# K and V of two chunks side by side in the array, a reordered prologue, and a tail that streams FFN products before out_proj

## The chip, the cores and the metric

The kernel runs on one core of one Trainium2 chip. Its time is the device time of that core in microseconds, as the median of a few runs; one further execution was recorded by the hardware profiler. Engines are PE (TensorE, matmuls), PEld (its weight loads), DVE (VectorE), ACT (ScalarE), POOL (GpSimd) and SP (SyncE, which issues most DMAs). Each engine takes its instructions strictly in the order written.

## What is computed

```python
x = A_x                                            # 1 x 2048 x 512
g = _sigmoid((x * gate_w).sum(-1, keepdims=True))
q = (x @ wq).reshape(B, S, 32, 16)                 # 32 heads of 16
k = x @ wk ; v = x @ wv                            # one K and V for all heads
p = _softmax(einsum("bhqd,bkd->bhqk", q, k) * 16 ** -0.5)
a = einsum("bhqk,bkd->bhqd", p, v).reshape(B, S, 512) @ wo
b = _silu(x @ w1) @ w2                             # w1: 512 x 1792
return g * a + (1 - g) * b
```

## The kernel before

Everything is float32 outside; inside, an operand is split into an upper and a lower float16 half (`split`: ACT makes the upper, DVE the lower), and a product is three matmuls (`product3`: upper x upper, upper x lower, lower x upper).

**Prologue** (`first_pass`). x comes in 4 chunks of 512 rows (`xn`). `T(c, t)` transposes 128 rows on PE and splits them into `xs`. `K(c)` multiplies a chunk by K's, V's and the gate's weights together (`wkvs`, 64 columns) into bank "pk", 12 matmuls 64 columns wide. `parts`/`place` split K and spread it over the partitions into `KT`; `v_rows`/`V` transpose V into `VF`. `W` splits the first half of wq, `Q(n)` makes one block of 128 columns of q for a chunk, writes it to memory (`qd`), and `load_q` reads it back rearranged into `qb`, by six DMAs plus two with the shift rows. `shift` makes a bound per head and query (`kab` times |q|) that stands in for the row maximum. `pieces_.step()` splits one piece of w1, w2, wq or wo, 128 x 512, that a DMA put into one of two buffers `raw`; a step asks for the load of a later piece into the buffer that it has emptied.

**Stream** (`attention`). 32 rounds (4 chunks, 4 blocks of 128 columns of q, 2 halves) of 16 steps, 512 steps; a step has two "scores" of 8 matmuls (`S<-qb,KT`, 32 columns each, eight tiles of the array at once). So there are 1024 scores, each followed by one exponential of 128 x 1024 on ACT (`P<-S`, L1180), in two pairs of PSUM banks: score n needs exponential n-2 done. The sums P x V are taken in one of two ways: native float32 (`pv<-P,VF`), or as two cheap products (`P,VP` and `L,VP`) for which DVE first makes `L` (L1199, 128 x 2048). Between scores a planner (`serve`, `put`, `f_slot`, with costs such as `SLOT` for a group of 8 matmuls) lays the FFN's and the output projection's products into banks "pm", of which there are two, and DVE's work by due times; the order is fixed when the program is built. `need(w, g)` puts all missing steps of a weight group on DVE at once.

The first scores are placed by hand, letter by letter, from `FIRST`: S is a score, E one matmul of an "early" Q block (blocks 4 and 5, 12 matmuls of 128 x 512 each, evicted by DVE at L929/L930), B is `bound` for block 1, which fetches the next FFN block and its "pm" bank first.

**Tail**. After the last score come the last sums, the last paired FFN products (48 matmuls at L835), the normalisation of the last round on DVE (`norm_a`, ending in `O`), then 72 full-height matmuls (L839): 12 of out_proj and 60 of the FFN, each block in a "pm" bank and evicted by DVE into `acc` (L809), which SP stores.

Of the kernel before, what the change touches and what calls it, by code (L numbers as in the profile page):

```python
# [31 lines left out]
FIRST = "EEEEEEEEEESEESEEEESEEEESBEEEE"  # L32
# [15 lines left out]
def kernel(  # L48
# [21 lines left out]
    nc = tc.nc  # L70
# [145 lines left out]
    def masks(cst):  # L216
# [6 lines left out]
        mj = cst.tile([16, 8, 16], F32)  # L223
        nc.gpsimd.iota(mj, pattern=[[0, 8], [1, 16]], base=0, channel_multiplier=-1, allow_small_or_imprecise_dtypes=True)
        sel_k = cst.tile([16, 8, 16], F32)
        nc.vector.tensor_scalar(flat(sel_k), flat(mj), 0.0, None, op0=OP.is_equal)
        selA = cst.tile([16, 8, 16], F16)
        selB = cst.tile([16, 8, 16], F16)
        nc.vector.memset(selA, 0.0)
        nc.vector.memset(selB, 0.0)  # L230
        for b in (0, 2, 4, 6):
            nc.vector.tensor_copy(selA[:, b], sel_k[:, b])
        for b in (1, 5):
            nc.vector.tensor_copy(selB[:, b], sel_k[:, b])
        part = cst.tile([128, 1], F32)
        nc.gpsimd.iota(part, pattern=[[0, 1]], base=0, channel_multiplier=1, allow_small_or_imprecise_dtypes=True)
        pm = cst.tile([128, 1], F32)
        nc.vector.tensor_scalar(pm, part, 64.0, -64.0, op0=OP.is_ge, op1=OP.mult)
        nc.vector.tensor_tensor(pm, pm, part, op=OP.add)
        rm = cst.tile([128, 2], F32)  # L240
# [15 lines left out]
    def load_q(q, c, o, rb, shifts):  # L256
# [3 lines left out]
        for f in range(2):  # L260
            b = 64 * f
            nc.sync.dma_start(q[b:b + 16], v[f, rb][:, :, 0])
            nc.sync.dma_start(q[b + 16:b + 32], v[f, rb][:, :, 0])
            nc.sync.dma_start(q[b + 32:b + 48], v[f, rb][:, :, 1])
            if shifts:
                nc.sync.dma_start(q[b + 48:b + 48 + shifts], u[f, rb][0:shifts])
        return q
# [22 lines left out]
    def loads(sb, q_cols):  # L290
# [7 lines left out]
        xn = []  # L298
        for c in range(NCH):
# [24 lines left out]
    def k_places(pk, k1, k2, selA, selB):  # L324

        nc.tensor.matmul(pk, flat(selA), k1, start=True, stop=False)
        nc.tensor.matmul(pk, flat(selB), k2, start=False, stop=True)
# [59 lines left out]
    def first_pass():  # L387
        with ExitStack() as pro:
# [8 lines left out]
            vr = sb.tile([64, S], F32)  # L397
            mx = sb.tile([16, NCH], F32)
            mxa = sb.tile([16, 1], F32)
            k_to = KS / (SX * SKV)  # L400
            ks = {}

# [4 lines left out]
            def K(c):  # L407
                ks[c] = bank("pk", 2)
                kv_product(ks[c], wkvs, c)

            def parts(c):
                pk = ks[c]
                k1, k2 = ks[c, "k"] = [wk_.tile([16, 512], F16, name=n) for n in ("k1", "k2")]
                nc.scalar.activation(k1, pk[0:16], AF.Copy, scale=k_to)
                absmax(mx[:, c:c + 1], k1)
                if c == NCH - 1:
                    nc.vector.tensor_reduce(mxa, mx, axis=AX.X, op=OP.max)
                nc.vector.scalar_tensor_tensor(k2, pk[0:16], k_to, k1, op0=OP.mult, op1=OP.subtract)

            def v_rows(c):  # L420
                nc.scalar.activation(vr[32:64, c * 512:c * 512 + 512], ks[c][32:64], AF.Copy)

            def place(c):
                pk = ps.tile([128, 512], F32, name="pt", bufs=4)
                k_places(pk, *ks[c, "k"], selA, selB)
                nc.scalar.activation(KT[:, c * 512:c * 512 + 512], pk, AF.Identity, bias=m_one)
# [24 lines left out]
            def shift(n, pu):  # L451
# [4 lines left out]
                if n == 0:  # L456

                    for p in range(2):
                        nc.sync.dma_start(qb_[0][48:113:64, p], s1[32 * p:32 * p + 3:2])
                return q_shift(o, c, s1)  # L460

            split(wkvs[:, 0], wkvs[:, 1], wkv, SKV)
            for m, a, n in (M_K, 0, 16), (M_V, 32, 16), (M_G, 48, 1):
                absmax(mxs[:, m:m + 1], wkvs[:, 0, :, a:a + n], AX.XY)
            T(0, 0, 1, 2, 3)
# [3 lines left out]
            T(1, 0, 1)  # L469
            K(0)  # L470
            T(1, 2, 3)
            T(2, 0)
            parts(0)
            T(2, 1)
            v_rows(0)
            K(1)
            place(0)
            T(2, 2, 3)
            T(3, 0)
            V(0)  # L480
            parts(1)
            T(3, 1)
            v_rows(1)
            W(0)
            W(1)
            K(2)
            pieces_.step(by_scalar=True)
            pieces_.step(by_scalar=True)
            place(1)
            T(3, 2, 3)  # L490
            V(1)
            parts(2)
            for _ in Q(0, pq):
                pass
            load_q(qb_[0], 0, 0, 0, 0)
            v_rows(2)
            pieces_.step(by_scalar=True)
            K(3)
            parts(3)
            place(2)  # L500
            q1 = Q(1, bank("pq", 1))
            next(q1)
            next(q1)
            prep = bank("pk", 2)
            nc.tensor.matmul(prep[:, 0:1], flat(sel_k), mxa, start=True, stop=True)
            kv_ = sb.tile([128, 1], F32)
            nc.vector.tensor_copy(kv_, prep[:, 0:1])
            nc.vector.tensor_scalar(kab, hmask, kv_, 2.0 ** -10 * (1 + 2.0 ** -9), op0=OP.mult, op1=OP.mult)
            v_rows(3)
            place(3)  # L510
            note = shift(0, bank("pk", 2))
            pieces_.step()

            lo = sb.tile([16, 2], F32)
            nc.vector.tensor_scalar(lo[:, 0:1], mxa, 0.5, None, op0=OP.is_lt)
            nc.vector.tensor_scalar(lo[:, 1:2], mxa, 6e4, None, op0=OP.is_gt)
            nc.vector.tensor_tensor(mxs[0:16, M_KK:M_KK + 1], lo[:, 0:1], lo[:, 1:2], op=OP.max)
            V(2)
            V(3)
            nc.vector.tensor_copy(VF[:, :, 0:16], pv_[:, :, 0:16])  # L520
            note()
            for _ in q1:
                pass
            sigmoid(pv_, -1.0 / (SX * SKV))
# [11 lines left out]
    def second_pass():  # L536
        with ExitStack() as pro:
# [61 lines left out]
            nc.tensor.matmul(prep[:, 0:1], flat(sel_k), km[0:16], start=True, stop=True)  # L599
# [137 lines left out]
    def attention(ctx, scale_of, t_scale, shifts, split_pieces, chores, q_todo, bounds, early, gates_, later):  # L737
# [356 lines left out]
        def norm_a(i, pv, rb, key):  # L1094
# [13 lines left out]
            def joined():  # L1108
# [10 lines left out]
                end = dve[0] + 1.9 if late else on_pool(4.0, dve[0]) + 2  # L1119
                put(0.84, end, end + 4, quotient)  # L1120

            def quotient():
# [5 lines left out]
                if rb:  # L1128
                    put(0.7, dve[0], dve[0] + 4, turned)
# [256 lines left out]
        while T_.cur or T_.going:  # L1386
            serve(pe[0])
            if not T_.going:
                nc.tensor.drain()
                for t in list(tasks):  # L1390
                    if t is T_.evicted:
                        do(t)
# [44 lines left out]
```

## Time and profile before

| what | us |
|---|---|
| median of 3 runs (lowest, highest) | 1075.2 (1071.62, 1076.59) |
| profiled execution, device time | 1073.23 |
| its span, first to last instruction | 1071.4 |
| first score on PE | 38.80 |
| last exponential ends | 1038.82 |
| last matmul ends | 1064.68 |
| last eviction by DVE ends | 1065.47 |

All times in the text count from the span's start. A row of a timeline is start, length, engine, line, operation, output<-inputs and count; the bracket at its end is the idle time of the engine before it and what ended it. A row of stretches has the stretch, its length, the busy time of each engine, the granted PE clock as a share of full speed, the DMA engines' share and GB/s.

### The profile page before, as it was taken

How to read it: one execution, taken by the hardware profiler on the slowest of the kernel's cores; microseconds unless marked ns; L12 is line 12 of the kernel's file. 1: busy time of each engine (PE TensorE's matmuls, PEld its weight loads, DVE VectorE, ACT ScalarE, POOL GpSimd, SP SyncE). 2: the span in 40 equal slices, each digit the busy share in tenths (PEclk: the TensorE clock that was granted, in tenths of full speed). 3: DMA queues.
4: the chain of work that ended last, by engine and by line, in shares of the span. 5: the costliest groups of instructions: out<-in, count | busy, mean ns of one | idle time of the engine just before them, and what ended most of it. 6: DMA issues, size and time to landing. Idle time of an engine off the chain costs nothing.

```text
span 1071.4 us, 65086 instructions
## 1 busy us (share of the span) xinstructions
PE 1023.1 (95%) x30610; PEld 564.2 (53%) x30610; DVE 916.6 (86%) x838; ACT 999.7 (93%) x1121; POOL 471.2 (44%) x388
## 2 busy tenths in 40 slices
PE   8999999999999999999999999999999999999996
PEld 5465454455555545455555555555555555555452
DVE  6799989999999998788797878888889898889784
ACT  5799999999999999999999999999999999999980
POOL 1034345324352373634744335465475267374620
PEclk9999999999999999999999999999999999999998
DMA  5421211100000100000000010000000010000001
GB/s 199 135 61 49 70 41 54 51 12 22 8 18 31 31 22 11 12 19 16 12 22 11 12 60 12 19 7 22 12 11 11 12 47 8 12 11 12 4 5 42
DMA packets 23079, 32.90 MB, mean 31 GB/s; under 512 B 5137, under 2 KB 13074, under 8 KB 22802
## 3 DMA queue, kind: packets, MB, share of 16 engines
q1 hardware_dynamic: 22050, 27.54, 8.4%
q8 instruction: 241, 3.95, 1.6%
q0 software_dynamic: 320, 1.05, 0.3%
q14 instruction: 36, 0.29, 0.1%
q10 hardware_dynamic: 432, 0.07, 0.0%
HBM read 20.12 MB, written 8.52 MB: 27 GB/s over the span
## 4 chain that ended last, share of the span: by engine, by line
PE 38%; ACT 35%; DVE 13%; issue 8%; POOL 4%; DMA 1%; ACTq 0%; SPq 0%; DVEq 0%; POOLq 0%
ACT P L1180 33%; PE pm L835 13%; PE pv L1278 12%; PE S L1174 9%; DVE L L1199 7%; PE pm L839 2%; ACT e L849 2%; POOL T L1109 1%; POOL U L1111 1%; DVE e L854 1%; PE pt L316 1%; DVE acc L809 1%; POOL T L1112 1%; POOL H L856 0%; POOL U L1116 0%
## 5 line engine op out<-in xcount | busy, mean ns | idle before, releaser
L1180 ACT ACTIVATE P<-S 128x1024 f32<-128x1024 f32 x1024 | 959.6, 1079 | 24.4 <-PE S L1174 22.7
L1199 DVE TENSOR_TENSOR L<-P 128x2048 f16<-128x2048 f32 x245 | 606.8, 2491 | 35.8 <-ACT P L1180 35.2
L1174 PE MATMUL S<-qb,KT 50*32 50x512 f16 x8192 | 435.0, 380 | 13.5 <-ACT P L1180 11.0
L1174 PEld LDWEIGHTS <-KT 50*32 50x32 f16 x8192 | 191.6, 89 | 244.5 <-issue 161.1
L1278 PE MATMUL pv<-P,VF 64*32 64x512 f32 (+1 forms) x5360 | 298.2, 503 | 0.0
L835 PE MATMUL pm<-xs,w1s 64*32 64x512 f16 x5376 | 263.7, 375 | 2.3 <-DVE e L854 1.1
L835 PE MATMUL pm<-w2s,H 64*32 64x512 f16 x4896 | 249.2, 375 | 4.9 <-DVE acc L807 2.0
L1109 POOL TENSOR_TENSOR T<-T,U 128x512 f32<-128x512 f32 x31 | 83.8, 2704 | 275.4 <-DVE U L1104 275.4
L856 POOL CAST H<-e 128x512 f16<-128x512 f32 x56 | 57.7, 1030 | 205.9 <-DVE e L854 204.3
L835 PEld LDWEIGHTS <-w1s 64*32 64x32 f16 x5376 | 116.1, 92 | 53.3 <-issue 14.9
L835 PEld LDWEIGHTS <-H 64*32 64x32 f16 x4896 | 106.2, 92 | 46.5 <-issue 6.3
L1278 PEld LDWEIGHTS pv<-P,VF 64*32 64x32 f32 x5360 | 104.7, 106 | 37.4 <-issue 6.6
L857 POOL TENSOR_TENSOR H<-e,H 128x512 f16<-128x512 f32 x56 | 108.8, 1943 | 4.5
L1278 PE MATMUL pv<-P,VP 64*32 64x512 bf16 x1952 | 108.1, 388 | 1.2 <-DVE U L1104 0.6
L1278 PE MATMUL pv<-L,VP 64*32 64x512 f16 x1952 | 103.3, 375 | 3.1 <-DVE L L1199 2.8
L1278 PEld LDWEIGHTS <-VP 64*32 64x32 f16 x3904 | 67.8, 93 | 45.1 <-issue 20.9
L835 PE MATMUL pm<-xs,wqs 64*32 64x512 f16 x1152 | 83.9, 375 | 1.1 <-DVE e L854 1.0
L854 DVE SCALAR_TENSOR_TENSOR e<-e,pm 128x512 f32<-128x512 f32 x56 | 38.3, 683 | 43.2 <-ACT e L849 42.9
L835 PE MATMUL pm<-wo_s,O 64*32 64x512 f16 x1440 | 68.3, 382 | 3.2 <-DVE acc L809 1.8
L1116 POOL TENSOR_TENSOR U<-U 128x48 f32<-128x48 f32 (+1 forms) x62 | 57.4, 925 | 2.4
L809 DVE SCALAR_TENSOR_TENSOR acc<-pm,g,acc 128x512 f32<-128x512 f32 x48 | 35.7, 744 | 14.6 <-PE pm L839 8.0
L1111 POOL TENSOR_TENSOR U<-T,mu 128x96 f32<-128x96 f32 x31 | 45.5, 1468 | 2.4
(175 smaller groups left out, 623.6 us busy)
## 6 DMA issues: line engine op xcount, KB each, us to landing
qb<-qd SPq DMA_DIRECT2D x192, 32.0 KB
raw<-in_B_w_dram SPq DMA_DIRECT2D x22, 256.0 KB
xn<-in_A_x_dram SPq DMA_DIRECT2D x8, 512.0 KB
out_dram<-acc SPq DMA_DIRECT2D x16, 256.0 KB
qd<-qx SPq DMA_DIRECT2D x12, 256.0 KB
raw<-in_B_w_dram POOLq DMA_DIRECT2D x4, 256.0 KB, 3.1
raw<-in_A_wo_dram SPq DMA_DIRECT2D x4, 256.0 KB
qb<-sh SPq DMA_DIRECT2D x62, 2.0 KB
```

Of the source, the lines that this page charges most:

```text
L809: nc.vector.scalar_tensor_tensor(a, po, gate[:, n:n + 1], a, op0=OP.mult, op1=OP.add)
L835: nc.tensor.matmul(self.bank[32 * m:32 * m + 32], l(i, rows, 32 * m), r(j, rows), start=first, stop=last)
L854: nc.vector.scalar_tensor_tensor(e, e, 1.0, ph, op0=OP.add, op1=OP.mult)
L856: nc.gpsimd.tensor_copy(H[:, 0], e)
L857: nc.gpsimd.tensor_tensor(H[:, 1], e, H[:, 0], op=OP.subtract)
L1109: eng.tensor_tensor(T, T, U, op=OP.add)
L1111: eng.tensor_tensor(z[:, :, 1:1 + DIGITS], T3[:, :, 17:17 + DIGITS], mu[:, :, 1:].to_broadcast([128, 16, DIGITS]), op=OP.mult)
L1116: eng.tensor_tensor(first, first, second, op=OP.add)
L1174: nc.tensor.matmul(sc[32 * m:32 * m + 32, f], KT[b:b + 50, k0:k0 + 32], qtile[i][b:b + 50, j], start=True, stop=True)
L1180: nc.scalar.activation(P[:, 2 * j:2 * j + 2], sc, AF.Exp, scale=scale_of(c, o))
L1199: nc.vector.tensor_tensor(L[s], P, upper(P), op=OP.subtract)
L1278: nc.tensor.matmul(pvs[i][h][32 * j:32 * j + 32, cols], a[r], b[r, j, cols], start=start, stop=rest == n)
```

## The change

1. **K and V.** `K(a)` takes chunks 2a and 2a+1: chunk 2a into columns 0 to 63 of the array (rows 0 to 63 of the bank), chunk 2a+1 into columns 64 to 127, alternating matmul by matmul. There are 48 matmuls as before, in 24 pairs. Splitting K, the absolute maximum and V's rows are done once for a pair, and V is turned by 8 plain matmuls instead of 16 transposes. The masks `sel_k`, `selA`, `selB` cover 128 partitions, and POOL makes selA and selB.
2. **The prologue's order.** wq is loaded between chunks 1 and 2 of x. Ten transposes come before the first K pair. Half of the six loads of `qb` for round 0 are issued by POOL, one of the two shift rows by ACT. Two of the four places of K are evicted by DVE. Two steps of w1 are made instead of four, both with ACT.
3. **The first scores.** `FIRST` begins with a score, and B stands after eleven early products instead of twenty.
4. **The tail.** Products are taken in the stream's order, in a ring of four halves of the scores' banks and two "pm" banks; out_proj comes when `O` is due by the plan.

```diff
-FIRST = "EEEEEEEEEESEESEEEESEEEESBEEEE"
+FIRST = "SEESEEESEEESEEESBEEESEEESEEESEEEE"
...
+            if c == 1:
+                nc.sync.dma_start(wqr, by_row(wq)[:, :, :q_cols])
             xn.append(t_)
-        wqr = sb.tile([128, KD, q_cols], F32)
-        nc.sync.dma_start(wqr, by_row(wq)[:, :, :q_cols])
...
-            def K(c):
-                ks[c] = bank("pk", 2)
-                kv_product(ks[c], wkvs, c)
...
+            def K(a):
+                pk = ks[a] = bank("pk", 2)
+                for kt in range(KD):
+                    for n, (i, j) in enumerate(((0, 0), (0, 1), (1, 0))):
+                        for h in range(2):
+                            c = 2 * a + h
+                            nc.tensor.matmul(pk[64 * h:64 * h + 64], wkvs[:, i, kt], xs[:, j, kt, c * 512:c * 512 + 512],
+                                             start=kt == n == 0, stop=kt == KD - 1 and n == 2)
...
-            def V(c):
-                for t in range(4 * c, 4 * c + 4):
-                    nc.tensor.transpose(pv_[:, t], vr[32:64, t * 128:t * 128 + 128], ident_[0][32:64, 32:64])
+            def V(a):
+                at = ident_[0].rearrange("p (h q n) -> p h q n", h=2, q=2)[:, :, 1]
+                for t in range(4):
+                    nc.tensor.matmul(pv_[:, 8 * a + t:8 * a + t + 5:4], vr[:, a, t * 128:t * 128 + 128], at, start=True, stop=True)
...
+            T(0, 0, 1)
             split(wkvs[:, 0], wkvs[:, 1], wkv, SKV)
+            T(0, 2, 3)
+            T(1, 0, 1, 2, 3)
...
+            T(2, 0, 1)
+            W(0)
+            W(1)
+            K(0)
+            T(2, 2, 3)
+            T(3, 0, 1, 2)
+            upper_k(0)
+            T(3, 3)
+            q0 = Q(0, pq)
...
+            load_q(qb_[0], 0, 0, 0, 0, nc.gpsimd)
+            K(1)
+            upper_k(1)
...
-        while True:
-            while tasks:
-                do(min(tasks, key=lambda t: t[0]))
-            o = ahead.pop() if ahead else fetch()
-            if o is None:
-                break
-            for n in range(o.n):
-                o.whole(n, n == 0, n == o.n - 1)
-            force(o.evict(o.bank))
+        def spaces():
+            while True:
+                for _ in range(2):
+                    sc = pS.tile([128, 2, 512], F32, name="S")
+                    yield sc[:, 0]
+                    yield sc[:, 1]
+                yield pM.tile([128, 512], F32, name="pm")
+                yield pM.tile([128, 512], F32, name="pm")
+
+        space = spaces()
+        while not ended[0] or tasks:
+            serve(pe[0])
+            o = ahead.pop() if ahead else next(seq, 0)
+            if o == 0:
+                ended[0] = True
+                while tasks:
+                    do(min(tasks, key=lambda t: t[0]))
+            elif o is None:
+                pe[0] += 0.05
+            else:
+                if not hasattr(o, "bank"):
+                    o.bank = next(space)
+                for n in range(o.n):
+                    o.whole(n, n == 0, n == o.n - 1)
+                    pe[0] += SLOT
+                o.evict(o.bank)
```

**What moves on DVE at the first early block.** `qs` is Q1's lower half, `raw_79` and `raw_80` are the two buffers of w1's pieces (L197 makes an upper half, L198 a lower), and `O<-pm` is the eviction of the first early block. Before:

```order
L197 TENSOR_SCALAR w1s<-raw_80 128x512
L198 SCALAR_TENSOR_TENSOR w1s<-raw_79,w1s 128x512
L198 SCALAR_TENSOR_TENSOR w1s<-raw_80,w1s 128x512
L515 TENSOR_SCALAR lo<-mxa 16x1
L516 TENSOR_SCALAR lo<-mxa 16x1
L517 TENSOR_TENSOR mxs<-lo 16x1
L520 COPY VF<-pv 128x16x16
L385 TENSOR_REDUCE um<-s_477 64x1
L119 SCALAR_TENSOR_TENSOR qs__508<-pq,qs__508 128x512
L929 TENSOR_SCALAR O<-pm 128x512
L930 SCALAR_TENSOR_TENSOR O<-pm,O 128x512
```

In the changed kernel, where the eviction's lines are L938 and L939:

```order
L198 SCALAR_TENSOR_TENSOR w1s<-raw_79,w1s 128x512
L119 SCALAR_TENSOR_TENSOR qs__477<-pq,qs__477 128x512
L137 TENSOR_REDUCE mxs<-wkvs 128x1 x3
L197 TENSOR_SCALAR w1s<-raw_79 128x512
L198 SCALAR_TENSOR_TENSOR w1s<-raw_80,w1s 128x512
L198 SCALAR_TENSOR_TENSOR w1s<-raw_79,w1s 128x512
L197 TENSOR_SCALAR w1s<-raw_80 128x512
L198 SCALAR_TENSOR_TENSOR w1s<-raw_80,w1s 128x512
L938 TENSOR_SCALAR O<-pm 128x512
L939 SCALAR_TENSOR_TENSOR O<-pm,O 128x512
```

Five steps of w1 now stand between Q1's half and the eviction; the first of them (L197 on raw_79) needs a third piece loaded by POOL, the fourth (L197 on raw_80) a fourth piece loaded by SP. The "pm" banks are handed out in turn: the first early block, then the FFN block that B fetches, then the second early block, whose first matmul (the thirteenth E) therefore waits for L939.

**What moves on SP at the same place.** `qd_0_91` is Q1's block on its way to memory, `qb_82` the queries of round 1. Before:

```order
L445 DMA qd_0_91<-qs__508 128x1024
L262 DMA qb_82<-qd_0_83 16x2x512
L263 DMA qb_82<-qd_0_83 16x2x512
L264 DMA qb_82<-qd_0_83 16x2x512
L266 DMA qb_82<-sh_0_84 1x2x512
...
L931 DMA qd_1_85<-O 128x1024
L180 DMA raw_79<-in_B_w_dram 128x512
```

Now:

```order
L458 DMA qd_0_91<-qs__477 128x1024
L262 DMA qb_82<-qd_0_83 16x2x512
L263 DMA qb_82<-qd_0_83 16x2x512
L264 DMA qb_82<-qd_0_83 16x2x512
L266 DMA qb_82<-sh_0_84 1x2x512
...
L180 DMA raw_80<-in_B_w_dram 128x512
L180 DMA raw_79<-in_B_w_dram 128x512
```

At the dots stand the other four loads of `qb_82`. The load of w1's fourth piece (raw_80) stands behind them; before, that piece had come by POOL ahead of them.

**What moves on DVE in the tail.** The last rows of O's chain and the evictions into `acc`; `gg` marks an out_proj block, `g_65` an FFN block. Before:

```order
L809 SCALAR_TENSOR_TENSOR acc<-pm,g_65,acc 128x512
L1124 RECIPROCAL rr<-T 128x16
L1127 TENSOR_TENSOR C<-T,rr 128x16x16
L1133 STREAM_TRANSPOSE T<-C 128x512
L1135 CAST O<-T 128x512
L1136 TENSOR_TENSOR O<-T,O 128x512
L809 SCALAR_TENSOR_TENSOR acc<-pm,gg,acc 128x512 x4
L809 SCALAR_TENSOR_TENSOR acc<-pm,g_65,acc 128x512 x7
```

Now:

```order
L1146 CAST O<-T 128x512
L1147 TENSOR_TENSOR O<-T,O 128x512
L818 SCALAR_TENSOR_TENSOR acc<-S,g_65,acc 128x512
L818 SCALAR_TENSOR_TENSOR acc<-S,gg,acc 128x512
L818 SCALAR_TENSOR_TENSOR acc<-S,g_65,acc 128x512
L818 SCALAR_TENSOR_TENSOR acc<-S,gg,acc 128x512
L818 SCALAR_TENSOR_TENSOR acc<-pm,gg,acc 128x512 x2
L818 SCALAR_TENSOR_TENSOR acc<-S,g_65,acc 128x512 x4
L818 SCALAR_TENSOR_TENSOR acc<-pm,g_65,acc 128x512
```

Two FFN blocks (24 matmuls on PE) now stand ahead of the four out_proj blocks (12), and five behind (36); the matmuls are the same 72.

In the stream the planner, fed with the new start, also lays the sums differently: 239 of 512 steps by the two cheap products and 273 native, before 244 and 268. From the thirteenth early product to score 12 (counted from 0) PE's order holds 12 early products, 8 scores and 4 whole native sums, and the first FFN product comes behind score 12; before, FFN products began after score 8, and by score 12 there were 12 groups of four FFN matmuls and three whole native sums.

More of the change, by code (lines that the diff above doesn't have):

```diff
@@ new lines, in first_pass @@
+            q1 = Q(1, bank("pq", 1))
+            place(0)
+            V(0)
+            next(q1)
+            prep = bank("pk", 2)
+            nc.tensor.matmul(prep[:, 0:2], flat(sel_k)[both], mxa[both], start=True, stop=True)
+            kv_ = sb.tile([128, 1], F32)
+            nc.vector.tensor_reduce(kv_, prep[:, 0:2], axis=AX.X, op=OP.max)
+            nc.vector.tensor_scalar(kab, hmask, kv_, 2.0 ** -10 * (1 + 2.0 ** -9), op0=OP.mult, op1=OP.mult)
+            lower_k(1)
+            place(1)
@@ L472, in first_pass @@
[L472 to L508, printed above, removed]
@@ L1118, in joined @@
                         eng.tensor_tensor(first, first, z[:, :, 3:4], op=OP.add)
-                end = dve[0] + 1.9 if late else on_pool(4.0, dve[0]) + 2
-                put(0.84, end, end + 4, quotient)
+                if late:
+                    dve[0] += 2.1
+                end = dve[0] if late else on_pool(4.0, dve[0]) + 2
+                put(0.7 if late else 0.84, end, end + 4 * (not late), quotient)
             def quotient():
@@ L1128, in quotient @@
                 if rb:
-                    put(0.7, dve[0], dve[0] + 4, turned)
+                    put(0.7, dve[0], dve[0] + 4 * (not late), turned)
             def turned():
```

144 lines of the change are left out of this document (79 added, 65 removed).

## The prediction

> **What bounds the kernel now.** I read the page's busy shares first, then the busy time by stretch, then the waits inside the long middle stretch.
>
> ```profile
> PE 1023.1 (95%) x30610; PEld 564.2 (53%) x30610; DVE 916.6 (86%) x838; ACT 999.7 (93%) x1121; POOL 471.2 (44%) x388
> ```
> ```profile
> 4.67:38.80 34.13, 33.53 (x174) 19.80 (x174) 24.43 (x60) 21.43 (x40) 2.75 (x6) 1.00 0.50 172
> ...
> 38.80:1038.82 1000.02, 967.60 (x30289) 535.19 (x30292) 874.94 (x747) 976.37 (x1079) 462.61 (x357) 1.00 0.09 25
> ...
> 1043.30:1051.60 8.30, 4.54 (x13) 1.53 (x14) 6.30 (x15) 0.00 (x0) 0.00 (x0) 0.79 0.00 1
> 1051.60:1064.70 13.10, 13.08 (x60) 5.75 (x59) 5.16 (x7) 0.00 (x0) 0.00 (x0) 1.00 0.11 41
> ```
>
> After each stretch come its length and the busy time of PE, PEld, DVE, ACT and POOL, then the granted clock. There are three regimes. Until the first scores at 38.80 PE works 33.5 of 34.1 us, so the prologue is PE's. In the stream PE (967.6 of 1000.0) and ACT (976.4) are both nearly full. In the tail PE works only 4.54 of the 8.30 us before 1051.60. Who is late in the stream, the waits tell (total, times, longest):
>
> ```profile
> ACT P L1180 <- PE S L1174: 22.7, 42, 1.4
> ...
> PE S L1174 <- ACT P L1180: 11.0, 30, 1.0
> ```
>
> ACT waits for scores 22.7 us and PE for exponentials 11.0 us: where one limits the other, it is PE two times in three (22.7 of 33.7).
>
> **Term 1, the prologue up to the end of Q1's product.** Scores and exponentials are numbered from 0. The timeline (start, length, engine, line, count):
>
> ```profile
> 11.50 0.38 PE L127 MATMUL pk<-xs,wkvs 128*64 128x512 f16 x1
> 11.71 0.38 PE L128 MATMUL pk<-xs,wkvs 128*64 128x512 f16 x1
> ...
> 36.34 0.38 PE L129 MATMUL pq<-xs,wqs 128*128 128x512 f16 x1
> ...
> 1019.52 0.41 PE L835 MATMUL pm<-wo_s,O 64*32 64x512 f16 x8
> ```
>
> and the chain of waits over the first 60 us:
>
> ```profile
> 13.67 0.61 ACT xs L118
> ...
> 14.30 1.30 DVE xs L119 x2
> 15.60 0.04 issue
> ```
>
> The K/V matmuls start 0.215 us apart, 48 of them 10.3 us. The last row is eight matmuls in eight tiles of the array in 0.41 us, as long as one (0.38). So I take the pairs to run side by side: 24 x 0.215 = 5.2 us, a saving of 5.2 (none, if they don't). V becomes 8 matmuls for 16; I give it nothing. Between 13.67 and 15.64 PE waits 2.0 us for ACT's and DVE's halves of the split; the new order puts ten transposes ahead of the first pair, but then DVE starves while that pair runs, so this is worth 2.0 at best and -1.0 at worst; I take 1. Q1's last matmul ends at 36.34 + 0.38 = 36.72 now, and would end at 30.5 (29.5 to 32.5, or 35.7 with pairs in turn). POOL's sel casts and the second DMA queues lie beside that.
>
> **Term 2, from Q1 to a steady stream.** Here the new order makes a wait. The first scores no longer stand behind ten early products. But the new FIRST puts its B behind eleven early products. B fetches an FFN block, which takes the second "pm" bank and calls `need`, so DVE gets five steps of w1 ahead of the eviction of the first early block. The 13th early product needs that bank, and it stands ahead of score 5. The fourth piece of w1 is loaded through SP, behind Q1's write and eight loads of qb. The price of this chain, from rows of before:
>
> ```profile
> 37.38 0.69 DVE L119 SCALAR_TENSOR_TENSOR qs__508<-pq,qs__508 128x512 f16<-128x512 f32 x1
> 39.79 0.69 DVE L929 TENSOR_SCALAR O<-pm 128x512 f16<-128x512 f32 x1 [1.71 <-PE pm L839]
> 40.52 0.69 DVE L930 SCALAR_TENSOR_TENSOR O<-pm,O 128x512 f16<-128x512 f32 x1
> ...
> 49.28 0.43 DVE L197 TENSOR_SCALAR w1s<-raw 128x512 f16<-128x512 f32 x1 [1.02 <-DMA raw<-in_B_w_dram]
> 49.74 0.69 DVE L198 SCALAR_TENSOR_TENSOR w1s<-raw,w1s 128x512 f16<-128x512 f32 x1
> ...
> 38.10 0.34 SPq L445 DMA_DIRECT2D qd<-qs__508  x1
> ...
> 42.74 0.35 SPq L931 DMA_DIRECT2D qd<-O  x1
> ...
> 46.43 0.33 SPq L180 DMA_DIRECT2D raw<-in_B_w_dram  x1
> ...
> 37.92 0.17 ACT L331 ACTIVATE gg<-pv 128x16 f32<-128x16 f32 x1
> 39.29 1.94 ACT L1180 ACTIVATE P<-S 128x1024 f32<-128x1024 f32 x2 [1.20 <-PE S L1174]
> ...
> 45.17 15.77 ACT L1180 ACTIVATE P<-S 128x1024 f32<-128x1024 f32 x17 [1.36 <-PE S L1174]
> ```
>
> From Q1's last matmul to the end of DVE's half of its split 1.35 (36.72 to 38.07); SP's write and eight loads 4.64 (38.10 to 42.74); the load of a piece 2.85 (46.43 to 49.28); its two DVE steps 1.15 (49.28 to 50.43); the eviction 1.42 (39.79 to 41.21). Sum 11.4, and some 0.4 more because ACT's two w1 halves now stand ahead of Q1's: 11.8. So the 13th early product starts at 30.5 + 11.8 = 42.3. ACT is free for exponentials 1.4 us after Q1 (36.72 to 38.09), with the 0.4 at 32.3, so the first comes 7 us sooner than now (39.29). They run 15.77 / 17 = 0.93 us apart; score 4 needs exponential 2 done, 32.3 + 3 x 0.93 = 35.1, and the 12th early product follows at about 35.5. From there PE stands still for about 7 us, and ACT runs dry behind it.
>
> What a stop does to PE's clock the tail of before shows, in the timeline and in stretches of half a us (clock third from the end):
>
> ```profile
> 1040.52 2.77 PE L835 MATMUL pm<-w2s,H 64*32 64x512 f16 x48
> 1046.83 4.63 PE L839 MATMUL pm<-wo_s,O 128*128 128x512 f16 x12 [3.54 <-DVE O L1135]
> 1051.57 13.11 PE L839 MATMUL pm<-w2s,H 128*128 128x512 f16 x60
> ```
> ```profile
> 1047.50:1048.00 0.50, 0.44 (x2) 0.17 (x3) 0.00 (x0) 0.00 (x0) 0.00 (x0) 0.50 0.00 0
> ...
> 1050.50:1051.00 0.50, 0.50 (x3) 0.25 (x2) 0.24 (x1) 0.00 (x0) 0.00 (x0) 0.72 0.00 0
> 1051.00:1051.50 0.50, 0.46 (x3) 0.10 (x1) 0.50 (x1) 0.00 (x0) 0.00 (x0) 1.00 0.00 0
> ```
>
> After 3.54 us of idling the granted clock stands at 0.50 from 1047.4 to 1050.8, 3.4 us, which loses 1.7 us of work. I charge the stop of 7 us the same 1.7. [...]
>
> From the 13th product to score 12 the new order holds 12 early products, 8 scores and 4 whole native sums. A native sum costs 0.86 us:
>
> ```profile
> 1017.13 1.04 PE L1278 MATMUL pv<-P,VF 64*32 64x512 f32 x16
> 1017.99 0.40 PE L1174 MATMUL S<-qb,KT 50*32 50x512 f16 x8
> ...
> 1038.12 0.42 PE L1278 MATMUL pv<-P,VP 64*32 64x512 bf16 x8
> 1038.34 0.41 PE L1278 MATMUL pv<-L,VP 64*32 64x512 f16 x8
> 1038.56 0.38 PE L835 MATMUL pm<-w2s,H 64*32 64x512 f16 x1
> ```
>
> 20 x 0.215 + 4 x 0.86 = 7.7, with the clock 9.4: exponential 12 starts at about 42.3 + 9.4 + 0.4 = 52.1. Now exponential 4 starts at 45.17, so 12 starts at 45.17 + 8 x 0.93 = 52.6. Of 7 us at score 0, 0.5 us are left at score 12. Bounds: 2.5 us lost to 2.5 us gained, by Q1's end and the clock.
>
> **Term 3, the rest of the stream.** The new order takes 239 steps by the two cheap products and 273 native, for 244 and 268. Each native step costs 0.86 for 0.44 (1038.12 to 1038.56): 5 x 0.42 = 2.1 us of PE. By score 12 the old order has issued 12 groups of FFN matmuls (2.6 us) and three native sums, the new one none and four: 1.7 us more to come. That is 3.8 us more PE work behind the same exponentials. PE is late two times in three: 2.5 us lost. Bounds: nothing, if all of it falls into PE's own waits, to 3.8.
>
> **Term 4, the tail.** PE now ends its paired products at 1040.52 + 2.77 = 1043.3, waits for O, takes 12 + 60 matmuls, and ends at 1051.57 + 13.11 = 1064.7. The new order puts two FFN blocks (24 matmuls, 5.2 us) where the wait was; O is ready 1046.83 - 1043.3 = 3.5 us in, so it hides. The 72 then run without a stop at full clock in 6 half-tiles and banks: 72 x 0.2155 = 15.5 for 21.4 us. Saving 5.9; I take 5.8. DVE's evictions (every 1.3 us at the end as now) stay behind PE. If one bank is late by one eviction, 4.5. What follows PE's end (last eviction, last store) stays.
>
> **Sum.** The profiled execution took 1073.23. It loses 0.5 (term 2 with 1), gains 2.5 (term 3), loses 5.8 (term 4): 1069.4. It lies 2.0 under the median of the three runs, 1075.2, whose range is 1071.6 to 1076.6; from the median the same sum gives 1071.4. I name 1070.4.
>
> **Rivals.**
> A: the stop at the 13th early product is short or absent, since a load lands sooner than 2.85 us after issue or SP is not behind. For: the 2.85 may hold some wait of DVE's. Then exponential 12 comes at 32.3 + 12 x 0.93 = 43.5 at best instead of 52.1; of these 8.6 us I count 7.4, since PE's backlog in term 3 grows with them: 1063. Chance 0.14.
> B: the pairs don't run side by side. Nothing in the trace shows two 64-column tiles at once. All of term 2 shifts by 5.2: 1075.6, no change. Chance 0.07.
> C, the slower side: after the stop PE stays at half clock. One score and three early products then cost 1.72 us for an exponential's 0.93. Each us at half clock loses 0.5. Slower by 0.5% is above 1080.6, 10.2 us over my sum, which holds 1.7 already: it decides from 24 us at half. At 28 us the time is 1070.4 + 14.0 - 1.7 = 1082.7. Against: 1051.00 is back at 1.00 after 3.4 us with PE less dense. Chance 0.07. [...]
>
> **Chances.** My forecast has 0.72, with an own range of 1066 to 1074. A run of this kernel can tell about 0.5% from no change, so "faster" is under 1069.8: 0.4 of the forecast's 0.72 and A, 0.43. "Slower" is C, 0.07. The rest, 0.50, is the same. The range reaches down to A and up past B, 1063 to 1076; C and the far side of A stay out.
>
> **What would show it.** Right: K/V pairs with two matmuls starting within 0.05 us and about 0.215 us a pair; Q1's last matmul near 30.5; first exponential near 32; a stop of PE near 35 to 42 before the 13th early product, put down to DVE's eviction, with DVE waiting for "raw" twice; granted clock 0.50 behind it; no idle PE between the paired products and the end of the tail. Wrong: exponentials going on past the fifth without a gap over 2 us (A), pairs 0.43 us apart (B), a clock row of 0.50 for over 10 us (C), or a stream from exponential 12 to the last that is longer or shorter than now by more than 4 us.

## The result: the tail's gain is there, and the new start gives all of it back

| kernel | median us (lowest to highest) | ratio to before, 95% interval |
|---|---|---|
| before | 1074.28 (1071.62 to 1077.49) | |
| after | 1074.72 (1072.91 to 1077.35) | 1.0005 [0.9995, 1.0015] |

The change makes no difference that can be measured. The profiled execution of after took 1077.35, the slowest of its twenty, 2.6 above its median; that of before (1073.23) lay 1.05 below its own. So places inside the run are compared here by their time from the span's start, and totals by medians.

The same views as in the prediction. The page's busy shares, and from the timeline the two K/V products and the end of the prologue:

```profile
PE 1023.3 (95%) x30674; PEld 566.1 (53%) x30674; DVE 900.7 (84%) x826; ACT 996.3 (93%) x1114; POOL 473.5 (44%) x397
```
```profile
12.80 1.20 PE L317 MATMUL pt<-ident,xn 128*128 128x128 f32 x8 [1.66 <-DMA xn<-in_A_x_dram]
...
13.93 2.78 PE L417 MATMUL pk<-xs,wkvs 128*64 128x512 f16 x24
...
22.67 2.78 PE L417 MATMUL pk<-xs,wkvs 128*64 128x512 f16 x24
...
29.96 1.41 DVE L436 TENSOR_SCALAR KT<-pt,m_one 128x512 f16<-128x512 f32 x2 [1.11 <-PE pt L328]
30.05 1.35 ACTq L472 DMA_DIRECT2D qb<-s  x1
...
31.45 0.60 ACT L430 ACTIVATE vr<-pk 128x512 f32<-128x512 f32 x1 [1.43 <-DVE KT L436]
...
32.10 1.60 PE L443 MATMUL pv<-ident,vr 128*128 128x64 f32 x8 [1.42 <-ACT vr L430]
...
34.34 0.63 PE L129 MATMUL pq<-xs,wqs 128*128 128x512 f16 x1
...
36.24 4.77 ACT L1193 ACTIVATE P<-S 128x1024 f32<-128x1024 f32 x5
```

24 K/V matmuls take 2.78 us: the pairs do run side by side. But Q1's last matmul ends at 34.97 (36.72 before), not at 30.5. Ahead of the first pair PE waits 1.66 us for chunk 2 of x, whose load now stands behind that of wq. Ahead of V(1) it waits 1.42 us for ACT's copy of V's rows, and that copy starts at 31.45, when two things have just ended: ACT's own DMA issue (30.05 + 1.35 = 31.40) and DVE's two evictions of KT (31.37), which the row names. Then the clock falls (stretches of 1 us; the clock is the third number from the end):

```profile
31.00:32.00 1.00, 0.00 (x0) 0.00 (x0) 0.37 (x1) 0.55 (x2) 0.00 (x0) 1.00 0.03 8
32.00:33.00 1.00, 0.90 (x6) 0.90 (x7) 0.00 (x0) 1.00 (x3) 0.00 (x0) 0.77 0.01 4
33.00:34.00 1.00, 1.00 (x6) 0.72 (x6) 0.27 (x1) 0.08 (x1) 0.00 (x0) 0.50 0.00 0
...
42.00:43.00 1.00, 0.00 (x0) 0.00 (x0) 0.00 (x0) 0.00 (x0) 0.00 (x0) 0.89 0.79 171
43.00:44.00 1.00, 0.00 (x0) 0.00 (x0) 0.17 (x1) 0.00 (x0) 0.00 (x0) 0.50 0.94 348
...
49.00:50.00 1.00, 1.00 (x11) 0.27 (x11) 0.00 (x0) 0.14 (x2) 0.00 (x0) 0.70 0.50 188
```

The second half-clock stretch, from about 42.8 to 49.6, lies around the stop before the 13th early product. The timeline there:

```profile
35.97 0.58 POOL L180 DMA_DIRECT2D raw<-in_B_w_dram  x1 [7.19 <-DVE w1s L198]
...
39.62 0.43 DVE L197 TENSOR_SCALAR w1s<-raw 128x512 f16<-128x512 f32 x1 [2.97 <-DMA raw<-in_B_w_dram]
...
40.45 0.55 SPq L266 DMA_DIRECT2D qb<-sh  x1
41.10 4.23 SPq L180 DMA_DIRECT2D raw<-in_B_w_dram  x3
43.83 0.43 DVE L197 TENSOR_SCALAR w1s<-raw 128x512 f16<-128x512 f32 x1 [2.57 <-DMA raw<-in_B_w_dram]
...
46.36 1.01 PE L848 MATMUL pm<-xs,wqs 128*128 128x512 f16 x2 [5.92 <-DVE O L939]
...
48.00 1.02 ACT L1193 ACTIVATE P<-S 128x1024 f32<-128x1024 f32 x1 [6.99 <-PE S L1187]
```

PE stands 5.92 us, ACT 6.99. And the tail, from the last paired products to the last eviction:

```profile
1049.61 2.77 PE L844 MATMUL pm<-w2s,H 64*32 64x512 f16 x48
1052.32 5.35 PE L848 MATMUL S<-w2s,H 128*128 128x512 f16 x24
1057.51 1.46 PE L848 MATMUL S<-wo_s,O 128*128 128x512 f16 x6
1058.80 1.46 PE L848 MATMUL pm<-wo_s,O 128*128 128x512 f16 x6
1060.47 6.64 PE L848 MATMUL S<-w2s,H 128*128 128x512 f16 x30 [0.21 <-DVE acc L818]
1066.94 1.46 PE L848 MATMUL pm<-w2s,H 128*128 128x512 f16 x6
```

The wait of 3.54 us for O is gone: from the end of the paired products to PE's end 16.0 us (1052.38 to 1068.40) for 21.4 before.

### The profile page after: what moved, and what is told of

It is laid out like the page before. It is cut to its first block, busy times and chain, and to the rows that moved or that the text cites. A ratio compares the mean times of both kernels' runs of the same rounds, so it can differ in the third digit from the quotient of the medians.

```text
span 1075.5 us, 65195 instructions
## 1 busy us (share of the span) xinstructions
PE 1023.3 (95%) x30674; PEld 566.1 (53%) x30674; DVE 900.7 (84%) x826; ACT 996.3 (93%) x1114; POOL 473.5 (44%) x397
## 4 chain that ended last, share of the span: by engine, by line
## 5 line engine op out<-in xcount | busy, mean ns | idle before, releaser
L1193 ACT ACTIVATE P<-S 128x1024 f32<-128x1024 f32 x1024 | 959.8, 1080 | 34.6 <-PE S L1187 32.5
L1212 DVE TENSOR_TENSOR L<-P 128x2048 f16<-128x2048 f32 x241 | 593.7, 2478 | 32.8 <-ACT P L1193 32.6
L1291 PE MATMUL pv<-P,VF 64*32 64x512 f32 (+1 forms) x5504 | 306.6, 501 | 0.0
L844 PE MATMUL pm<-xs,w1s 64*32 64x512 f16 x5376 | 261.0, 375 | 2.7 <-DVE e L863 2.1
L844 PE MATMUL pm<-w2s,H 64*32 64x512 f16 x4896 | 246.4, 375 | 4.9 <-DVE acc L818 2.0
L1118 POOL TENSOR_TENSOR T<-T,U 128x512 f32<-128x512 f32 x31 | 96.0, 3097 | 308.0 <-DVE U L1113 308.0
L865 POOL CAST H<-e 128x512 f16<-128x512 f32 x56 | 69.3, 1238 | 186.9 <-DVE e L863 181.8
L1291 PEld LDWEIGHTS pv<-P,VF 64*32 64x32 f32 x5504 | 108.7, 106 | 37.1 <-issue 5.1
L866 POOL TENSOR_TENSOR H<-e,H 128x512 f16<-128x512 f32 x56 | 117.8, 2103 | 4.5
L1291 PEld LDWEIGHTS <-VP 64*32 64x32 f16 x3824 | 67.5, 93 | 42.8 <-issue 18.6
L863 DVE SCALAR_TENSOR_TENSOR e<-e,pm 128x512 f32<-128x512 f32 x56 | 38.2, 683 | 49.3 <-ACT e L858 49.1
L844 PEld LDWEIGHTS <-wqs 64*32 64x32 f16 x1152 | 35.6, 93 | 15.8 <-issue 6.3
L818 DVE SCALAR_TENSOR_TENSOR acc<-pm,g,acc 128x512 f32<-128x512 f32 x42 | 31.3, 745 | 13.7 <-PE pm L844 13.6
```

What stands on the lines that cost most here:

```text
L818: nc.vector.scalar_tensor_tensor(a, po, gate[:, n:n + 1], a, op0=OP.mult, op1=OP.add)
L844: nc.tensor.matmul(self.bank[32 * m:32 * m + 32], l(i, rows, 32 * m), r(j, rows), start=first, stop=last)
L863: nc.vector.scalar_tensor_tensor(e, e, 1.0, ph, op0=OP.add, op1=OP.mult)
L865: nc.gpsimd.tensor_copy(H[:, 0], e)
L866: nc.gpsimd.tensor_tensor(H[:, 1], e, H[:, 0], op=OP.subtract)
L1118: eng.tensor_tensor(T, T, U, op=OP.add)
```

## The experiments

Places of each profiled execution, us from its start. Exponential 12 is taken inside a merged row at even spacing. The last two columns are the stretch from exponential 12 to the end of the last exponential, and from there to the end of the last eviction. "Late bound" is after with B behind all early products; "both mends" has the shift row off ACT as well.

| kernel | median us | ratio to before | Q1 ends | exp. 0 | exp. 12 | stream | tail |
|---|---|---|---|---|---|---|---|
| before | 1074.28 | | 36.72 | 39.29 | 52.6 | 986.2 | 26.65 |
| after | 1074.72 | 1.0005 [0.9995, 1.0015] | 34.97 | 36.24 | 56.9 | 990.8 | 21.51 |
| e1 tail alone | 1067.33 | 0.9938 [0.9917, 0.9960] | 36.62 | 39.19 | 52.5 | 988.3 | 20.93 |
| e2 all but the tail | 1080.47 | 1.0060 [1.0039, 1.0080] | 33.20 | 34.47 | 56.8 | 987.6 | 27.91 |
| e3 late bound | 1064.91 | 0.9911 [0.9891, 0.9931] | 34.53 | 35.80 | 49.1 | 988.9 | 20.92 |
| e4 no DMA on ACT | 1072.88 | 0.9987 [0.9973, 1.0001] | 31.71 | 32.98 | 55.0 | 988.7 | 21.51 |
| e5 both mends | 1065.53 | 0.9919 [0.9894, 0.9944] | 32.05 | 33.32 | 46.5 | 988.6 | 20.92 |
| e6 w1 by POOL | 1073.42 | 0.9995 [0.9982, 1.0008] | 33.72 | 34.98 | 57.5 | 986.3 | 21.50 |
| e7 K apart, both mends | 1067.12 | 0.9932 [0.9913, 0.9950] | 35.53 | 36.80 | 49.9 | 989.7 | 20.93 |
| e8 old E/S order, both mends | 1062.00 | 0.9890 [0.9869, 0.9912] | 32.03 | 34.60 | 49.3 | 989.2 | 15.39 |
| e9 old FIRST in after | 1077.69 | 1.0035 [1.0022, 1.0048] | 33.29 | 35.85 | 55.8 | 990.0 | 21.97 |
| e10 both mends again | 1063.60 | 0.9897 [0.9875, 0.9919] | 32.52 | 33.79 | 46.9 | 988.2 | 20.92 |
| e11 late bound again | 1066.35 | 0.9922 [0.9902, 0.9942] | 34.44 | 35.71 | 49.1 | 991.8 | 20.92 |
| e12 w1 earlier | 1069.54 | 0.9959 [0.9946, 0.9972] | 33.61 | 34.88 | 49.7 | 987.5 | 24.56 |

Where `FIRST` or the prologue's steps differ, the planner also lays the stream anew. Counted in the traces, 239 of the 512 sums are made by the two cheap products in after, e2, e4 and e6, 234 in e3, e5, e7, e10 and e11, 237 in e8, 238 in e9 and 233 in e12. So a comparison across these groups moves more than the letters that the edit names.

**The two halves of the change.** e1 is before with the new tail: the last loop of the diff, with the plan's due times for O. e2 is after with the old one.

```diff
 e1, in before
+                if not hasattr(o, "bank"):
+                    o.bank = next(space)
...
-            force(o.evict(o.bank))
+                o.evict(o.bank)
```

> The kernel before with the new tail alone; prologue and early order stay as they were. Theory 1 (the tail gains what the two traces show, 26.65 us from the last exponential to the last eviction before against 21.5 after, and the new prologue gives it back): 1074.3 - 5.1 = about 1069.2. Theory 2 (neither part moves the end, since what the tail saves comes back as later evictions and stores): within 1 us of 1074.3.

> The changed kernel with the old tail: new prologue and early order alone. Theory 1: slower than before by what the tail gains, 1074.3 + 5.5 = about 1079.8, with exponential 12 near 56.6 us and the last one some 8 us later than before. Theory 2: within 1 us of 1074.3. Theory 3 (the two parts don't add up, because the profiled run of the changed kernel was its slowest): between them, 1075 to 1078.

The tail alone gains 0.62% (0.40 to 0.83), 6.7 us, and the rest alone loses 0.60% (0.39 to 0.80), 6.4 us. The two are equal and add up to the result; theory 2 (neither matters) and theory 3 (1075 to 1078) fall. In e2 exponential 12 comes at 56.8, as in after: 4.2 of the 6.4 us are lost before the stream gets going. The last exponential comes 5.7 us later than before, where 8 was expected, and e2's tail is 1.3 us longer than that of before.

**The stop before the 13th early product.** e3 moves B; e12 leaves it and makes the first two w1 steps earlier, with a third behind them; e6 leaves it and sends the early loads of w1 by POOL.

```diff
 e3
-FIRST = "SEESEEESEEESEEESBEEESEEESEEESEEEE"
+FIRST = "SEESEEESEEESEEESEEESEEESEEESEEEEB"
 e12
+            pieces_.step(by_scalar=True)
             place(0)
             V(0)
+            pieces_.step(by_scalar=True)
             next(q1)
...
             nc.vector.tensor_tensor(mxs[:, M_KK:M_KK + 1], lo[:, 0:1], lo[:, 1:2], op=OP.max)
-            pieces_.step(by_scalar=True)
 e6
-        split_pieces.queue = nc.sync
         blocks = [(c, g) for c in range(NCH) for g in range(len(GF))]
...
+        split_pieces.queue = nc.sync
         if later:
```

> The changed kernel with the bound (B) behind the 24 early products instead of ahead of the 13th. Theory 1 (the stop before the 13th product costs the stream what it costs the early exponentials): no PE wait over 2 us there, exponential 12 near 47 to 49 us instead of 56.6, and half to all of the 7 us and of the half clock behind it arrives at the end: 1074.7 - 4 to - 8 = 1067 to 1071. Theory 2 (PE is the bound for the rest of the stream and its work is unchanged, so early exponentials only make PE's queue longer): exponential 12 is early, the last one is not, 1073 to 1075. Price against theory 1: DVE's five w1 steps now fall among the exponential's low parts.

> The changed kernel with the bound where it is, but three w1 steps in the prologue instead of two, the first two of them 5 to 8 us sooner (ahead of and behind the first chunk's place), so that the loads of the third and the fourth piece go out near 27 and 33 instead of 36 and 41. Theory 1 (the stop is the loads' latency, one after the other through two buffers): the 13th early product comes 4 to 6 us sooner than 46.36, at about 40.5 to 42.5, and the time falls to 1066 to 1071. Theory 2 (the DVE steps and SP's queue make the stop, whenever the loads land): the 13th product within 1.5 us of 46.36 and 1073.5 to 1075.5.

> The changed kernel with the bound where it is; only the loads of w1's pieces during the early products go out on POOL's queue instead of SP's, past the 8 loads of the second round's q. Theory 1, the link that the prediction put into the chain (the piece waits 4.6 us behind SP's write and loads): the 13th early product comes 2 to 4 us sooner than 46.36 and the time falls by 1 to 3. Theory 2, from the trace after (POOL's load, issued at 35.97, lands only at 39.6, when SP is almost through; only 0.5 us of waiting is SP's): the 13th product at 45.9 to 47, time 1074 to 1076.

The timeline of e3; the 12th to the 14th early product are its last row:

```profile
35.80 8.19 ACT L1193 ACTIVATE P<-S 128x1024 f32<-128x1024 f32 x8
...
39.54 0.82 PE L848 MATMUL pm<-xs,wqs 128*128 128x512 f16 x3
```

No FFN block has taken the second bank, so the 13th product waits for no eviction. Eight exponentials run without a gap, exponential 12 comes 7.8 us sooner than in after and the median is 9.8 us lower, by its later runs (e11) 8.4. Theory 1 holds, and the gain is somewhat above its range: the stop is worth all it costs ACT. What comes on top of the 7.8 is not explained: e3's tail is 0.6 us shorter, and its stream is laid otherwise. In e12, with B where the change has it:

```profile
39.10 0.69 DVE L939 TENSOR_SCALAR O<-pm 128x512 f16<-128x512 f32 x1 [2.28 <-PE pm L849]
...
40.57 0.59 PE L849 MATMUL pm<-xs,wqs 128*128 128x512 f16 x2 [1.51 <-DVE O L940]
```

The wait falls from 5.92 to 1.51 us and the time to 1069.54, inside theory 1's range: what stops PE is that the third and fourth piece of w1 are asked for too late. (e12 also has three rows of w1 on DVE ahead of this eviction instead of five. They can't be what counts: the two rows fewer are worth 1.15 us, and DVE now stands idle for 2.28.) Exponential 12 comes about as early as in e3, but the time is 4.6 us above that of e3; of this the tail explains 3.6, since 84 full-height matmuls are left for it instead of 72. In e6 the chain to the eviction of the first early block is no shorter:

```profile
40.57 1.08 POOL L180 DMA_DIRECT2D raw<-in_B_w_dram  x2 [4.66 <-ACT P L1192]
...
43.48 0.43 DVE L197 TENSOR_SCALAR w1s<-raw 128x512 f16<-128x512 f32 x1 [2.88 <-DMA raw<-in_B_w_dram]
...
45.27 0.69 DVE L938 SCALAR_TENSOR_TENSOR O<-pm,O 128x512 f16<-128x512 f32 x1
```

The eviction ends at 45.96, 12.2 us after Q1's end, and in after at 46.30, 11.3 us after it; the time is not told apart from that of after. In after DVE has emptied the buffer at about 40.6 and SP is through with its loads at 41.00, so SP's queue holds the fourth piece for 0.4 us, not 4.6. What makes the chain long is two loads one behind the other, each waiting for a buffer that DVE empties: 35.97 to 39.62 and 41.10 to 43.83.

**The wait for V's rows.** e4 issues both shift rows on SP.

```diff
-                    for p, queue in enumerate((nc.sync, nc.scalar)):
+                    for p, queue in enumerate((nc.sync, nc.sync)):
```

> The changed kernel with both of Q0's shift rows issued on SP; ACT issues none. Theory 1 (ACT's DMA issue, 1.35 us at 30.05, holds ACT's copy of V's rows and so V(1) and Q1): the copy starts near 30.1, V(1) without a wait near 30.7, the clock stays at 1.00, Q1's last matmul ends near 31 to 32 instead of 34.97, and the first exponential comes 2 to 3 us sooner; 1071.5 to 1073.5. Theory 2 (the copy waits for DVE's two evictions of KT, as the named releaser says, which end at 31.37): nothing moves but the issue, 1074.7 +- 0.7.

Its timeline at the same place:

```profile
28.84 0.59 ACT L468 ACTIVATE s<-pk 64x512 f16<-64x512 f32 x1 [0.39 <-PE pk L379]
...
29.33 0.58 ACT L430 ACTIVATE vr<-pk 128x512 f32<-128x512 f32 x1
29.37 1.41 DVE L436 TENSOR_SCALAR KT<-pt,m_one 128x512 f16<-128x512 f32 x2 [1.11 <-PE pt L328]
29.45 1.19 SPq L472 DMA_DIRECT2D qb<-s  x2
...
29.96 1.10 PE L443 MATMUL pv<-ident,vr 128*128 128x64 f32 x8
```

ACT's copy starts the moment its own work before is done, while DVE's evictions of KT have only begun. The releaser that the row in after names was the wrong one; ACT's own issue was the hold. Q1 ends at 31.71. The time falls by 1.8 us, inside theory 1's range, but the intervals of the two ratios just overlap. The stop stands behind this: the 13th early product still waits 7.23 us and comes at 44.39, so of the 3.26 us by which Q1 ends sooner 1.97 arrive there. (One of twelve executions of e4 took 5875.87 us. The ratio leaves it out; the median counts it and would be 1072.77 without it. No trace shows it, and its cause is open.)

**Both mends, and what then bounds.** e5 and e10 are one kernel, e3 and e11 another.

```diff
-FIRST = "SEESEEESEEESEEESBEEESEEESEEESEEEE"
+FIRST = "SEESEEESEEESEEESEEESEEESEEESEEEEB"
...
-                    for p, queue in enumerate((nc.sync, nc.scalar)):
+                    for p, queue in enumerate((nc.sync, nc.sync)):
```

> The changed kernel with the bound behind the 24 early products and both shift rows on SP. Theory 1 (the two waits stand in line, ACT's DMA issue ahead of Q1's end and the stop behind it, and each is paid by itself): Q1's last matmul ends at 31.7 as with the shift rows alone, exponential 0 at 33, exponential 12 at about 49.1 - 2.8 = 46.3, and the time is 1064.9 - 1.8 to - 3.3 = 1061.6 to 1063.1. Theory 2 (PE's own work to exponential 12 bounds it once the stop is gone): 1064 to 1065.5.

> The kernel with both mends again, beside the one with the late bound alone. Theory 1 (ACT's DMA issue costs as much when the stop is gone as with it): 1.8 to 3.3 us faster than the late bound alone. Theory 2 (PE's own work bounds from there on, and the earlier start is lost as idle time among the early products): within 1 us of it.

> The late bound alone, with the shift row on ACT, once more, to stand beside the kernel with both mends on one chip: 1064 to 1066 by its first runs; theory 1 puts it 1.8 to 3.3 us above the kernel with both mends, theory 2 within 1 us.

Exponential 12 comes 2.6 and 2.2 us sooner than in the late bound alone, as theory 1 says. At the end this isn't told apart. e5's 1065.53 is at the upper end of theory 2, while e10 lies in theory 1's range below e11: e5 lies 0.6 above e3, e10 2.75 below e11 on one chip; all twelve runs of each give a mean difference of -1.4, with an interval of about 1.8 either way. Whether ACT's issue still costs once the stop is gone stays open.

**The pairs.** e7 runs the chunks of a pair one after the other, with both mends.

```diff
-                for kt in range(KD):
-                    for n, (i, j) in enumerate(((0, 0), (0, 1), (1, 0))):
-                        for h in range(2):
-                            c = 2 * a + h
+                for h in range(2):
+                    c = 2 * a + h
+                    for kt in range(KD):
+                        for n, (i, j) in enumerate(((0, 0), (0, 1), (1, 0))):
```

> As the kernel with both mends, but K and V's 24 matmuls of a pair of chunks run one chunk after the other (12, then 12) instead of alternating between the column halves. Theory 1 (the halves run side by side: 24 matmuls in 2.78 us instead of 24 x 0.2155 = 5.2): each of the two products takes 2.4 us more; the second stands on PE's path whole and the first too if PE is not waiting for x then: Q1's end 2.4 to 4.8 us later and the time 2.4 to 4.8 us longer than the kernel with both mends. Theory 2 (the pairs are no faster than one after the other, or it is hidden): the same within 0.7 us.

```profile
13.65 4.53 PE L417 MATMUL pk<-xs,wkvs 128*64 128x512 f16 x24
...
24.14 4.53 PE L417 MATMUL pk<-xs,wkvs 128*64 128x512 f16 x24
```

4.53 us for 2.78, and Q1 ends 3.5 us later than in e5 (35.53 for 32.05), which is twice the difference: both products stand on PE's path. Exponential 12 is 3.4 us later. The medians differ by 1.6, less than the 2.4 to 4.8 of theory 1, and the intervals overlap: what the pairs are worth at the end is not shown. 24 matmuls in turn would be 5.2 at 0.215 apart; the trace has eight starts in the half us where one chunk gives way to the next, for four to six in those around it, so the halves overlap a little even there.

**The order of scores and early products.** e8 is e5 with the letters E and S as before and B last; e9 is after with the FIRST of before, word for word.

```diff
 e8, in e5
-FIRST = "SEESEEESEEESEEESEEESEEESEEESEEEEB"
+FIRST = "EEEEEEEEEESEESEEEESEEEESEEEEB"
 e9, in after
-FIRST = "SEESEEESEEESEEESBEEESEEESEEESEEEE"
+FIRST = "EEEEEEEEEESEESEEEESEEEESBEEEE"
```

> As the kernel with both mends, but the early products stand in the old order (10 of them ahead of the first score, 4 scores among the 24), with the bound last as there. Theory 1 (ACT's exponentials set the pace of the early part, so the scores between the products count): exponential 0 comes 1.3 us later, ACT runs dry among the products, exponential 12 comes 2 to 5 us later, and so does the end. Theory 2 (PE's work to exponential 12 is the same and bounds it): exponential 12 and the time within 0.7 us of the kernel with both mends.

> The changed kernel with the early order of before, word for word: 10 products ahead of the first score, 4 scores among the 24, the bound behind the 20th; shift row on ACT as in the change. Theory 1 (what stops PE is that the bound comes ahead of the first block's eviction on DVE, not the w1 steps as such): the eviction stands ahead of them again, no PE wait over 2 us before the 13th product, and the time is that of the kernel with both mends and this order, 1062.0, plus what ACT's issue costs, 0 to 3: 1062 to 1065. Theory 2 (the w1 steps, two fewer in the prologue, stop PE wherever the bound stands): the stop moves behind the 20th product, 1068 to 1073.

Both expectations for e8 missed: exponential 12 comes 2.8 us later than in e5, as theory 1 has it, but the end doesn't; its median is the lowest of all, though its interval overlaps with that of e10. The tail shows what makes up for the 2.8:

```profile
1043.27 4.06 PE L848 MATMUL S<-w2s,H 128*128 128x512 f16 x18
1049.24 1.11 PE L848 MATMUL S<-wo_s,O 128*128 128x512 f16 x3 [1.91 <-DVE O L1146]
1050.19 1.46 PE L848 MATMUL pm<-wo_s,O 128*128 128x512 f16 x6
1051.49 0.81 PE L848 MATMUL S<-wo_s,O 128*128 128x512 f16 x3
```

Thirty full-height matmuls are left for the tail instead of 72; the stream took the other 42 among its own products, and the tail is 5.5 us shorter, though the last exponential comes 3.4 us later than in e5. By the pages of the profile PE is busy for 1015.7 us in e8 and 1021.2 in e5, while between its first and last matmul it stands idle for 31 us in e8 and 28 in e5. So e8 is ahead by less work on PE, not by shorter stops. How much of that the order of the letters makes and how much the planner's other layout is not shown.

e9 went wrong in size for both theories. PE does not stop before the 13th product (theory 1), but the stop has moved (theory 2) to the first FFN product, which waits for the bound's shift behind the w1 steps. The timeline, and the clock in stretches of 2 us:

```profile
49.11 0.62 PE L844 MATMUL pm<-xs,w1s 64*32 64x512 f16 x4 [3.89 <-DVE qx L1086]
```
```profile
46.00:48.00 2.00, 0.00 (x0) 0.00 (x0) 1.69 (x5) 0.42 (x1) 0.00 (x0) 1.00 0.66 238
48.00:50.00 2.00, 0.89 (x20) 0.40 (x23) 1.41 (x4) 0.00 (x0) 0.00 (x0) 0.50 0.66 169
...
56.00:58.00 2.00, 2.00 (x46) 1.22 (x38) 1.40 (x3) 0.96 (x2) 0.00 (x0) 0.50 0.00 1
58.00:60.00 2.00, 2.00 (x71) 1.51 (x56) 1.79 (x11) 1.69 (x2) 0.00 (x0) 0.94 0.24 64
```

The clock stays at half from 48.0 to about 58.2, and PE works through 9.1 us of that, which loses 4.6. Exponential 12 is 6.6 us later than in e8, and the rest 7.3 us longer; of that the tail explains 6.6 (21.97 for 15.39). Which of the two differences from e8 (B four products earlier, the shift row on ACT), and how much of it the planner's other layout, stays open.

## Why the prediction was right, and where not

**The answer** (no change the likeliest, 1070.4 in 1063 to 1076) held, but the sum behind it did not come out. 1074.72 is 4.3 us above the named 1070.4 and outside the forecast's own range of 1066 to 1074. It lies in the wider range because that reaches up past rival B (1075.6), whose mechanism did not come: in that the answer was lucky. From the profiles: the tail saves 5.1 in after and 5.7 in e1, where 5.8 was forecast; exponential 12 comes 4.3 us later, where 0.5 sooner was forecast; the stream from there is longer by 4.6 in this profile, where 2.5 was forecast.

**Term 1 is the step that failed.** The pairs run side by side, as taken. But Q1's end came at 34.97, 4.5 us behind the forecast and outside its range (29.5 to 32.5). Without the DMA on ACT it is 31.71, inside it. The prediction had set the second DMA queues "beside that", at nothing, without naming who stands behind the issue on ACT: the copy of V's rows, V(1), Q1's fourth quarter. From the first K/V matmul to Q1's end it is 18.4 us in e4, e5 and e10; 19.9 in e2, e6, e9 and e12, with ACT's issue and the clock at full to Q1's end; 20.7 to 21.0 in after, e3 and e11, where the clock falls. So the issue costs 1.55 us and the clock another 0.8 to 1.1. What is left of the 4.5 is a first K/V matmul that comes 0.6 us later in after than in e4, and 1.2 that e4 lacks too (31.71 for 30.5). For these the prediction read 13.67 to 15.64 as a wait of PE that the new order could spare, 1 us of it. That stretch is on the chain, but PE was transposing in it, and waited 0.24:

```profile
12.89 2.19 PE L316 MATMUL pt<-ident,xn 128*128 128x128 f32 x16
...
15.64 0.38 PE L128 MATMUL pk<-xs,wkvs 128*64 128x512 f16 x1 [0.24 <-DVE xs L119]
```

From its first matmul to Q1's end PE stands idle 0.6 us in before, so there was no wait of 1 us to spare. The new order has waits of its own: for chunk 2 of x, 0.79 us in e4 and 1.66 in after. That wq's load, now ahead of it, causes them is likely, but no run moves it back.

**Term 2.** The stop is where it was forecast and as long: 11.4 us from Q1's end to the 13th product, for 11.8. The length was right in part by luck. The sum went by SP's queue alone, 6.4 us from Q1's end to the issue of the fourth piece (1.35, 0.4 and 4.64), and it is 6.1 in after (34.97 to 41.10). But a second path, which the sum doesn't have, is nearly as long: POOL's load of the third piece, 3.65 us, and DVE's steps free the buffer at about 40.6. So SP's queue is worth 0.4, and e6, without it, was no sooner. Most of term 1's error arrives at the 13th product, 46.36 for 42.3, and at exponential 12, 56.9 for 52.1. The clock was at half for 6.8 us, not 3.4, but PE stood idle for the first 3.6 of them; the loss is 1.6, for 1.7 forecast.

**Term 3.** After, e2, e4 and e6 share one order from the 13th product on and take 986.3 to 990.8 from exponential 12 to the last; before and e1 share another and take 986.2 and 988.3. The means differ by 1.1, less than one order's own spread. The 2.5 is neither shown nor excluded. In the profile of after the stretch is 4.6 us longer than before, past the 4 us that the prediction named as a sign against it; in e2, e4 and e6 it is 0.1 to 2.5 longer.

**Term 4** held: with the paired products' end as the mark, 15.6 us in e1 and 16.0 in after, for 15.5 forecast. The forecast reserve of one late bank came as 0.21 us.

**The rivals.** A (no stop) did not come, and e3 shows what it would have been worth: 1064.9, where 1063 was forecast. B (pairs in turn) falls. C did not come in after, but e9 shows its mechanism: half a clock for 10 us with PE at work, which the prediction took to end after 3.4.

**The clock.** The charge of 1.7 us rested on one stretch, the 3.4 us at 0.50 behind 3.54 us of idling in before's tail, and the room that the bounds leave for the clock was an estimate that no run shows. After shows 3.4 us at 0.50 (32.5 to 35.9) behind a wait of 1.42 and 6.8 at the stop. That wait of 1.42 us before V(1) stands in after, e2, e3, e6, e9, e11 and e12; in four of the seven the clock halves within 3 us, in three it doesn't; in the five profiles of the new prologue without it (e4, e5, e7, e8 and e10) it never does there. What decides whether it falls behind such a gap, and for how long, is not shown.

## What to carry to other kernels

A DMA that is moved to a working engine's queue is an instruction on that engine (here 1.35 us of ACT's queue, and 1.55 at Q1's end): write down what stands behind it and who waits for that, even for one transfer of two rows. Where a fetch puts work ahead of an eviction, count the loads that the work has yet to ask for, one latency for each turn of its buffers (here 3.65 us from issue to use and then 2.73). And a mark inside the run is not the end: e8 reaches exponential 12 2.8 us later than e5 and did not end later. Where a planner lays the rest anew, compare what is left for the tail and how long the fullest engine is busy as well.

## What was not expected of the hardware

Of the two equal transfers of two rows of the shift, SP issued one in 0.65 us and ACT the other in 1.35 (30.04 and 30.05, in after); SP issued both in 1.19 in e4. The named releaser of a wait was wrong by a whole engine where two ends lay 0.03 us apart. And stretches at half clock measured 3.4 us (before's tail), 6.8 (after's stop) and 10.2 (e9): about one, two and three times the same length.
